# Attention row sums on VectorE and GpSimd, with P^T stored chunk-innermost, in place of ones-matmuls on TensorE

## The chip, the cores and the metric

The kernel runs on one core of one Trainium2 chip. The metric is the device time of one execution in microseconds (us), as the median of several executions. The profile's span is a little shorter than that time (366.2 us against 368.0 us for the profiled execution of the kernel before), because it runs from the first to the last instruction.

## The reference, cut to what matters

Two independent problems A and B, each a grouped-query attention block with a cache:

```python
# B=16, Sq=32, D=1024, Hq=32, Hkv=4, Sk=512, Dh=128, all bf16
q = (x @ wq)                                  # 32 query heads of 128
scores = einsum("bhqd,bhkd->bhqk", q, k) * Dh ** -0.5   # 8 query heads share one k head
p = softmax(scores, axis=-1)
o = einsum("bhqk,bhkd->bhqd", p, v)
out = o.reshape(B, Sq, Hq * Dh) @ wo          # both problems concatenated on the last axis
```

## The kernel before

The kernel works in 128 slots, one for each (batch, key head) of both problems. A slot holds the scores transposed: the 512 keys lie on the 128 partitions in KC = 4 chunks, and the QW = 256 columns are 8 heads x 32 queries. So a softmax row sum is a sum over 4 chunks and over 128 partitions. P^T below is the tile `p_sb`, the exponentials in this transposed form. In `nc.tensor.matmul` the `lhsT` argument is called the stationary operand and `rhs` the moving operand; SBUF and PSUM are the names of the two memories in which the kernel places its tiles. Around the attention work of a slot, TensorE is fed with seven "units", single 512-column matmuls of the projections (Q first, then the output projection).

```python
def scores(i):
    ...
    s_ps = psum.tile([P, KC, QW], FP32, name="s_ps", tag="s")
    for c in range(KC):
        nc.tensor.matmul(s_ps[:, c, :], lhsT=kT[:, i % GRP, c, :], rhs=<q of the 8 heads>, ...)
    p_sb = work.tile([P, KC, QW], BF16, name="p_sb", bufs=3)         # chunk-outermost
    nc.scalar.activation(out=p_sb[:], in_=s_ps[:], func=ACTF.Exp, bias=shift[:], scale=SCALE)

def partial_sums(i):                       # VectorE: sum of the 4 chunks
    nc.vector.tensor_tensor(out=t1[:], in0=p_sb[:, 0:2, :], in1=p_sb[:, 2:4, :], op=ALU.add)
    nc.vector.tensor_tensor(out=t[:], in0=t1[:, 0, :], in1=t1[:, 1, :], op=ALU.add)

def values(i):
    ob = psum.tile([P, 2 * QW], FP32, name="ob", tag="ob")
    for c in range(KC):
        nc.tensor.matmul(ob[:, 0:QW], lhsT=v_sb[:, i % GRP, c, :], rhs=d["p"][:, c, :], ...)
    nc.tensor.matmul(ob[:, QW:2 * QW], lhsT=ones[:], rhs=d["t"][:], start=True, stop=True)  # sum over partitions
    nc.scalar.activation(out=lg[:, q, :], in_=ob[:, QW:2 * QW], func=ACTF.Ln)
    nc.scalar.activation(out=r[:], in_=lg[:, q, :], func=ACTF.Exp, scale=-1.0)              # 1 / sum
    ...

for i in range(2 * NG):                    # 128 slots
    do_loads(i); scores(i); run(units, 4)
    if i > 0: values(i - 1)
    partial_sums(i); run(units, 3)
    if i > 0: normalize(i - 1)             # VectorE: ob * r -> oT
```

At the end a check value is read and a branch skips a slow general path, which these inputs never take.

Of the kernel before, what the change touches and what calls it, by code (L numbers as in the profile page):

```python
# [24 lines left out]
SHIFT = 44.0  # L25
ONES = 2.0 ** -75
LIMIT = 20.0
# [145 lines left out]
def kernel(  # L173
# [26 lines left out]
    BPT = P // SQ  # L200
    QW = REP * SQ

    out_flat = out.flatten_outer_dims()
# [5 lines left out]
    def fast_path(ok_i):  # L209
        with ExitStack() as fctx:  # L210
            enter = fctx.enter_context
            const = enter(tc.tile_pool(name="const", bufs=1))
            blk = enter(tc.tile_pool(name="blk", bufs=20))
            kv = enter(tc.tile_pool(name="kv", bufs=2))
# [3 lines left out]
            enter(tc.manual_schedule())  # L218

            nc.scalar.preload_act_table_set("natural_log_exp_and_others")  # L220

# [3 lines left out]
            ident = const.tile([P, P], BF16, name="ident")  # L225
            make_identity(nc, ident[:])
            ones_f = const.tile([P, P], FP32, name="ones_f")
            nc.vector.memset(ones_f[:], ONES)
            ones = const.tile([P, P], FP32R, name="ones")
            nc.vector.tensor_copy(out=ones[:], in_=ones_f[:])  # L230
            one_col = const.tile([P, 1], FP32, name="one_col")
# [4 lines left out]
            nc.vector.memset(cnt[:], 0.0)  # L236
            NLR = 2 * NG // GRP
            lall = const.tile([NLR, GRP * QW], FP32, name="lall")

# [25 lines left out]
            def load_kv(j):  # L265
                pr, jj = divmod(j, NG // GRP)
                k, v = problems[pr][1], problems[pr][2]
                kT = kv.tile([P, GRP, SK], BF16, name="kT")
                v_sb = kv.tile([P, GRP, KC, DH], BF16, name="v_sb")
                if pr == 0:  # L270
                    g, b0 = divmod(jj * GRP, B)
                    ks, vs = k[b0:b0 + GRP, g], v[b0:b0 + GRP, g]
                    for q in range(GRP):
                        nc.sync.dma_start_transpose(out=kT[:, q, :], in_=ks[q])
                else:
                    ks, vs = k[jj], v[jj]
                    nc.sync.dma_start_transpose(
                        out=kT[:], in_=ks.rearrange("g k d -> (g k) d")
                    )
                nc.sync.dma_start(  # L280
                    out=v_sb[:], in_=vs.rearrange("q (p c) d -> p q c d", c=KC)
                )
                kv_tiles[j] = (kT, v_sb)
# [26 lines left out]

            def f_units(pr, tt, nh, last=False):
                ps = psum.tile([P, NW], FP32, name="f_ps", tag="proj")
                for h in range(HQ):
                    nc.tensor.matmul(  # L314
                        ps[:],
                        lhsT=oT[pr, tt][:, h, :],
                        rhs=wo_tiles[pr, nh, h // REP][:, h % REP, :],
                        start=(h == 0),
                        stop=(h == HQ - 1),
                    )  # L320
                    if h == HQ - 1:
                        o_sb = outp.tile([P, NW], BF16, name="o_sb")
                        nc.vector.tensor_copy(out=o_sb[:], in_=ps[:])  # L323
                        c0 = problems[pr][5] + nh * NW
                        (nc.sync if last else nc.gpsimd).dma_start(  # L325
                            out=out_flat[tt * P:(tt + 1) * P, c0:c0 + NW], in_=o_sb[:]
                        )
                    yield
# [16 lines left out]
            def scores(i):  # L345
# [3 lines left out]
                for c in range(KC):  # L349
# [6 lines left out]
                    )  # L356
                p_sb = work.tile([P, KC, QW], BF16, name="p_sb", bufs=3)
                nc.scalar.activation(  # L358
                    out=p_sb[:], in_=s_ps[:], func=ACTF.Exp, bias=shift[:], scale=SCALE
                )  # L360
                st[i] = {"p": p_sb}

            def partial_sums(i):
                p_sb = st[i]["p"]
                t1 = work.tile([P, 2, QW], FP32, name="t1")
                nc.vector.tensor_tensor(
                    out=t1[:], in0=p_sb[:, 0:2, :], in1=p_sb[:, 2:4, :], op=ALU.add
                )
                t = work.tile([P, QW], FP32R, name="t")
                nc.vector.tensor_tensor(  # L370
                    out=t[:], in0=t1[:, 0, :], in1=t1[:, 1, :], op=ALU.add
                )
                st[i]["t"] = t

            ltile = {}

            def values(i):
                d = st[i]
                v_sb = kv_tiles[i // GRP][1]
                ob = psum.tile([P, 2 * QW], FP32, name="ob", tag="ob")  # L380
                for c in range(KC):
                    nc.tensor.matmul(  # L382
                        ob[:, 0:QW],
                        lhsT=v_sb[:, i % GRP, c, :],
                        rhs=d["p"][:, c, :],
                        start=(c == 0),
                        stop=(c == KC - 1),
                    )
                nc.tensor.matmul(  # L389
                    ob[:, QW:2 * QW], lhsT=ones[:], rhs=d["t"][:], start=True, stop=True  # L390
                )
                d["ob"] = ob
                j, q = divmod(i, GRP)
                if q == 0:
                    ltile[j] = work.tile([P, GRP, QW], FP32, name="lg")
                lg = ltile[j]
                nc.scalar.activation(  # L397
                    out=lg[:, q, :], in_=ob[:, QW:2 * QW], func=ACTF.Ln
                )
                r = work.tile([P, QW], FP32, name="r")  # L400
                nc.scalar.activation(out=r[:], in_=lg[:, q, :], func=ACTF.Exp, scale=-1.0)  # L401
                d["r"] = r
                if q == GRP - 1:
                    nc.gpsimd.dma_start(  # L404
                        out=lall[j:j + 1, :],
                        in_=lg[0:1, :, :].rearrange("p q n -> p (q n)"),
                    )

            def normalize(i):
                pr, b, g = where(i)  # L410
                d = st.pop(i)
                tt, bl = divmod(b, BPT)
                if (pr, tt) not in oT:
                    oT[pr, tt] = blk_tile([P, HQ, P], "oT")
                nc.vector.scalar_tensor_tensor(  # L415
                    out=oT[pr, tt][:, g * REP:(g + 1) * REP, bl * SQ:(bl + 1) * SQ],
                    in0=d["r"][:].rearrange("p (h s) -> p h s", s=SQ),
                    scalar=ONES,
                    in1=d["ob"][:, 0:QW].rearrange("p (h s) -> p h s", s=SQ),
                    op0=ALU.mult,  # L420
                    op1=ALU.mult,
                )
# [70 lines left out]
            def stream():  # L493
# [4 lines left out]
                for nh in range(NH):  # L498
                    for tt in range(TT):
                        yield from f_units(0, tt, nh)  # L500
                for tts in ((0, 1), (2,)):
                    for nh in range(NH):
                        for tt in tts:
                            yield from f_units(1, tt, nh)
                for nh in range(NH):
                    yield from f_units(1, TT - 1, nh, last=(nh == NH - 1))

# [9 lines left out]
            for j in range(2, 2 * NG // GRP):  # L517
                at(GRP * (j - 1) + 1, load_kv, j)
            for c4 in range(3, 16):
# [7 lines left out]
            at(12, load_xT_b)  # L527
            for nh in range(NH):
                for hg in range(HKV):
                    at(NG - 12 + nh * 8 + hg * 2, load_wo, 0, nh, hg)  # L530
                    at(NG + 20 + nh * 18 + hg, load_wo, 1, nh, hg)

# [4 lines left out]

            for i in range(2 * NG):
                do_loads(i)
                scores(i)  # L540
                run(units, 4)
                if i > 0:
                    values(i - 1)
                partial_sums(i)
                run(units, 3)
                if i > 0:
                    normalize(i - 1)
            run(units, 4)
            values(2 * NG - 1)
            run(units, 4)  # L550
            normalize(2 * NG - 1)


            run(units, 8)
            sq = blk_tile([NLR, GRP * QW], "sq", FP32)
            nc.vector.tensor_tensor(out=sq[:], in0=lall[:], in1=lall[:], op=ALU.mult)
# [15 lines left out]
                        skip_runtime_bounds_check_because="only compared")  # L572
    with tc.If(ok < total, preferred_fallthrough_block=False):
        general_path(tc, problems, out_flat)
# [30 lines left out]
```

## Time and profile before

| what | before |
|---|---|
| time, median | 368.9 us (at the prediction: 368.77 us) |
| PE busy | 97% of the span |
| VectorE, ScalarE busy | 67%, 68% |
| slot period (timeline) | 2.52 us |

The page of the kernel before: its first part (busy us, share, instructions), its part 4 (the chain that ended last, by engine), and rows of its part 5 (line, engine, operation, out<-in, count, busy us, mean ns of one).

```profile
PE 356.6 (97%) x2236; PEld 225.0 (61%) x2236; DVE 244.2 (67%) x478; ACT 249.2 (68%) x389; POOL 25.1 (7%) x53
...
PE 97%; DVE 0%; ACT 0%; issue 0%
...
L358 ACT ACTIVATE p_sb<-s_ps,shift 128x1024 bf16<-128x1024 f32 x128 | 142.7, 1115 | 47.5 <-PE s_ps L350 47.5
...
L382 PE MATMUL ob<-p_sb,v_sb 128*128 128x256 bf16 x512 | 76.8, 273 | 0.0
L350 PE MATMUL s_ps<-qT,kT 128*128 128x256 bf16 x512 | 76.8, 273 | 0.0
...
L389 PE MATMUL ob<-t,ones 128*128 128x256 f32 x128 | 46.5, 363 | 0.0
```

The timeline of PE in the kernel before (start us, duration us of the merged run, engine, line, operation, count).

```profile
200.36 0.60 PE L350 MATMUL s_ps<-qT,kT 128*128 128x256 bf16 x4
200.80 1.03 PE L314 MATMUL f_ps<-wo_sb,oT 128*128 128x512 bf16 x4
201.66 0.60 PE L382 MATMUL ob<-p_sb,v_sb 128*128 128x256 bf16 x4
202.02 0.36 PE L389 MATMUL ob<-t,ones 128*128 128x256 f32 x1
202.22 0.82 PE L314 MATMUL f_ps<-wo_sb,oT 128*128 128x512 bf16 x3
202.88 0.60 PE L350 MATMUL s_ps<-qT,kT 128*128 128x256 bf16 x4
```

How to read this: a matmul's mean of 273 ns is how long one takes, but they are pipelined, and what counts is the distance between starts. Four score matmuls occupy the array from 200.36 to 200.80, 0.44 us, 0.11 us each; four value matmuls and the ones-matmul together occupy 201.66 to 202.22, 0.56 us. One slot lasts from 200.36 to 202.88, 2.52 us. PE never waits in the loop (its only wait is 1.2 us, at the start), so TensorE is the bound. Busy time is a poor measure of what matmuls cost here: the ones-matmuls' 46.5 us of busy time are 4.2% of the chain, 15.4 us.

VectorE had one reducing instruction of the size that the change needs, 1024 elements, at the end of the kernel before (timeline of DVE):

```profile
349.40 1.21 DVE L557 TENSOR_SCALAR_CACHE_REDUCE sq<-sq 32x1024 f32<-32x1024 f32 x1
```

### The profile page before, as it was taken

The page shows a single profiled execution, that of the slowest core. Times are in us where ns is not written, and L with a number is a line of the kernel's source. Part 1 is how long each engine was busy: PE and PEld are TensorE (multiplying, and loading weights), DVE is VectorE, ACT ScalarE, POOL GpSimd, SP SyncE. Part 2 cuts the span into 40 slices and gives each one's busy share as a digit, 9 for nine tenths or more (in the row PEclk, how much of TensorE's full clock was granted, in tenths as well). Part 3 has the DMA queues.
Part 4 walks back from the last instruction along what each step waited for, and adds up shares of the span by engine and source line. Part 5 has one row for each costly group of instructions (what it writes and reads, how often), then busy time and mean ns, then how long its engine had stood idle before and what let it go on. Part 6 is the DMA issues. An engine that isn't in the chain of part 4 may idle for free.

```text
span 366.2 us, 6094 instructions
## 1 busy us (share of the span) xinstructions
PE 356.6 (97%) x2236; PEld 225.0 (61%) x2236; DVE 244.2 (67%) x478; ACT 249.2 (68%) x389; POOL 25.1 (7%) x53
## 2 busy tenths in 40 slices
PE   8999999999999999999999999999999999999990
PEld 5556666666666666666666666666666666666540
DVE  2458788887878787888856666666666676666530
ACT  3037777777777777777777777777777777777500
POOL 0000000000000000000001110110001111011100
PEclk9999999999999999999999999999999999999998
DMA  8998796977777784999995555799548974440000
GB/s 274 301 280 242 225 264 147 243 225 219 184 194 183 220 201 115 314 304 310 314 305 138 130 131 142 207 352 198 139 113 287 315 194 117 131 129 17 15 16 21
DMA packets 125974, 71.91 MB, mean 196 GB/s; under 512 B 74641, under 2 KB 124945, under 8 KB 125937
## 3 DMA queue, kind: packets, MB, share of 16 engines
q1 hardware_dynamic: 122848, 68.30, 67.5%
q0 software_dynamic: 1744, 2.10, 2.4%
q10 hardware_dynamic: 1344, 1.05, 0.9%
q8 instruction: 19, 0.31, 0.4%
q14 instruction: 19, 0.15, 0.1%
HBM read 51.38 MB, written 2.10 MB: 146 GB/s over the span
## 4 chain that ended last, share of the span: by engine, by line
PE 97%; DVE 0%; ACT 0%; issue 0%
PE f_ps L314 31%; PE q_ps L297 30%; PE s_ps L350 15%; PE ob L382 15%; PE ob L389 4%; PE warm_ps L446 1%; PE q_ps L469 1%; PE xT_ps L455 0%; ACT xT L460 0%; DVE o_sb L323 0%; DVE xT L459 0%; DVE warm L224 0%; PE ok_ps L563 0%
## 5 line engine op out<-in xcount | busy, mean ns | idle before, releaser
L358 ACT ACTIVATE p_sb<-s_ps,shift 128x1024 bf16<-128x1024 f32 x128 | 142.7, 1115 | 47.5 <-PE s_ps L350 47.5
L314 PE MATMUL f_ps<-wo_sb,oT 128*128 128x512 bf16 x512 | 132.8, 380 | 0.0
L297 PE MATMUL q_ps<-xT,wq_sb 128*128 128x512 bf16 x496 | 128.4, 380 | 0.0
L382 PE MATMUL ob<-p_sb,v_sb 128*128 128x256 bf16 x512 | 76.8, 273 | 0.0
L350 PE MATMUL s_ps<-qT,kT 128*128 128x256 bf16 x512 | 76.8, 273 | 0.0
L397 ACT ACTIVATE lg<-ob 128x256 f32<-128x256 f32 x128 | 49.5, 387 | 39.8 <-PE ob L389 39.8
L350 PEld LDWEIGHTS <-kT 128*128 128x128 bf16 x512 | 57.0, 113 | 28.3 <-issue 0.2
L382 PEld LDWEIGHTS <-v_sb 128*128 128x128 bf16 x512 | 50.1, 98 | 33.1
L314 PEld LDWEIGHTS <-oT 128*128 128x128 bf16 x512 | 44.6, 98 | 32.9
L297 PEld LDWEIGHTS <-wq_sb 128*128 128x128 bf16 x496 | 43.4, 97 | 31.9
L401 ACT ACTIVATE r<-lg 128x256 f32<-128x256 f32 x128 | 53.6, 418 | 4.0
L305 DVE CAST qT<-q_ps 128x512 bf16<-128x512 f32 x62 | 42.7, 689 | 18.2 <-PE q_ps L297 18.0
L415 DVE SCALAR_TENSOR_TENSOR oT<-r,ob 128x256 bf16<-128x256 f32 x128 | 53.5, 418 | 1.6 <-ACT r L401 1.6
L389 PE MATMUL ob<-t,ones 128*128 128x256 f32 x128 | 46.5, 363 | 0.0
L404 POOL DMA_DIRECT2D lall<-lg x32 | 15.9, 496 | 245.4 <-ACT lg L397 245.4
L389 PEld LDWEIGHTS ob<-t,ones 128*128 128x128 f32 x128 | 24.3, 190 | 1.4
L323 DVE CAST o_sb<-f_ps 128x512 bf16<-128x512 f32 x16 | 11.0, 689 | 9.0 <-PE f_ps L314 9.0
L325 POOL DMA_DIRECT2D out_dram<-o_sb x15 | 8.6, 571 | 81.3 <-DVE o_sb L323 81.3
L460 ACT COPY xT<-xT_ps 128x512 bf16<-128x512 bf16 x4 | 2.1, 590 | 5.1 <-DVE xT L459 5.1
L459 DVE COPY xT<-xT_ps 128x512 bf16<-128x512 bf16 x4 | 1.7, 426 | 5.3 <-PE xT_ps L455 5.3
L446 PE MATMUL warm_ps<-warm 128*128 128x512 bf16 x10 | 4.0, 560 | 1.2 <-DVE warm L224 1.2
L469 PE MATMUL q_ps<-xT,wq_sb 128*128 128x256 bf16 x32 | 4.0, 272 | 0.1
(280 smaller groups left out, 158.5 us busy)
## 6 DMA issues: line engine op xcount, KB each, us to landing
v_sb<-in_A_v_cache_dram SPq DMA_DIRECT2D x16, 512.0 KB, 4.2
wq_sb<-in_B_wq_dram SPq DMA_DIRECT2D x8, 1024.0 KB, 6.3
wo_sb<-in_A_wo_dram SPq DMA_DIRECT2D x8, 1024.0 KB, 7.5
v_sb<-in_B_v_cache_dram SPq DMA_DIRECT2D x16, 512.0 KB, 4.2
wo_sb<-in_B_wo_dram SPq DMA_DIRECT2D x8, 1024.0 KB, 8.9
wq_sb<-in_A_wq_dram SPq DMA_DIRECT2D x7, 1024.0 KB, 7.1
out_dram<-o_sb POOLq DMA_DIRECT2D x15, 128.0 KB, 2.4
kT<-in_A_k_cache_dram SPq DMA_TRANSPOSE x64, 3.1
```

The costliest lines, as they stand in the source:

```text
L297: nc.tensor.matmul(ps[:], lhsT=w[:, dc, (h % 4) * DH:(h % 4 + 1) * DH], rhs=xT[pr][:, dc, :], start=(dc == 0), stop=(dc == DC - 1),)
L305: nc.vector.tensor_copy(out=qT[pr, g][:, :, hl, :], in_=ps[:].rearrange("p (b s) -> p b s", s=SQ),)
L314: nc.tensor.matmul(ps[:], lhsT=oT[pr, tt][:, h, :], rhs=wo_tiles[pr, nh, h // REP][:, h % REP, :], start=(h == 0), stop=(h == HQ - 1),)
L323: nc.vector.tensor_copy(out=o_sb[:], in_=ps[:])
L350: nc.tensor.matmul(s_ps[:, c, :], lhsT=kT[:, i % GRP, c, :], rhs=qT[pr, g][:, b, :, :].rearrange("p h s -> p (h s)"), start=True, stop=True,)
L358: nc.scalar.activation(out=p_sb[:], in_=s_ps[:], func=ACTF.Exp, bias=shift[:], scale=SCALE)
L382: nc.tensor.matmul(ob[:, 0:QW], lhsT=v_sb[:, i % GRP, c, :], rhs=d["p"][:, c, :], start=(c == 0), stop=(c == KC - 1),)
L389: nc.tensor.matmul(ob[:, QW:2 * QW], lhsT=ones[:], rhs=d["t"][:], start=True, stop=True)
L397: nc.scalar.activation(out=lg[:, q, :], in_=ob[:, QW:2 * QW], func=ACTF.Ln)
L401: nc.scalar.activation(out=r[:], in_=lg[:, q, :], func=ACTF.Exp, scale=-1.0)
L404: nc.gpsimd.dma_start(out=lall[j:j + 1, :], in_=lg[0:1, :, :].rearrange("p q n -> p (q n)"),)
L415: nc.vector.scalar_tensor_tensor(out=oT[pr, tt][:, g * REP:(g + 1) * REP, bl * SQ:(bl + 1) * SQ], in0=d["r"][:].rearrange("p (h s) -> p h ...
```

## The change

The intent is to take the ones-matmul off the bound engine. P^T is stored with the four chunks innermost, `[P, QW, KC]`, so that VectorE sums the chunks in one reduce over contiguous elements; GpSimd, almost idle before, sums over the partitions for two slots at a time; Ln and the reciprocal run once for two slots; the value matmuls and everything that waits for the sums run four slots behind (LAG = 4). The value matmuls must then read every fourth bf16 element of P^T, a step of 8 bytes. Besides, the last output is written in two halves, the branch at the end gets a hint, the identity matrix is built on VectorE instead of GpSimd, the logarithms kept for the check are stored from ScalarE's queue, and loads are scheduled a little differently.

```diff
-                p_sb = work.tile([P, KC, QW], BF16, name="p_sb", bufs=3)
+                p_sb = work.tile([P, QW, KC], BF16, name="p_sb", bufs=LAG + 2)
                 nc.scalar.activation(
-                    out=p_sb[:], in_=s_ps[:], func=ACTF.Exp, bias=shift[:], scale=SCALE
+                    out=p_sb[:], in_=s_ps[:].rearrange("p c n -> p n c"), func=ACTF.Exp, bias=shift[:], scale=SCALE
                 )
 ...
-                nc.vector.tensor_tensor(
-                    out=t1[:], in0=p_sb[:, 0:2, :], in1=p_sb[:, 2:4, :], op=ALU.add
-                )
 ...
-                nc.vector.tensor_tensor(
-                    out=t[:], in0=t1[:, 0, :], in1=t1[:, 1, :], op=ALU.add
-                )
 ...
+                nc.vector.tensor_reduce(
+                    out=tsum[j][:, q, :],
+                    in_=p_sb[:],
+                    axis=AX.X,
+                    op=ALU.add,
+                )
+                if q == 1:
+                    sums[j] = work.tile([P, 2, QW], FP32, name="sums", bufs=3)
+                    nc.gpsimd.partition_all_reduce(
+                        sums[j][:].rearrange("p q n -> p (q n)"),
+                        tsum.pop(j)[:].rearrange("p q n -> p (q n)"),
+                        channels=P,
+                        reduce_op=bass_isa.ReduceOp.add,
+                    )
 ...
+            def reciprocals(j):
+                lg = sums.pop(j)
+                nc.scalar.activation(out=lg[:], in_=lg[:], func=ACTF.Ln, scale=DOWN)
+                rcp[j] = work.tile([P, 2, QW], FP32, name="r")
+                nc.scalar.activation(out=rcp[j][:], in_=lg[:], func=ACTF.Exp, scale=-1.0)
 ...
                     nc.tensor.matmul(
-                        ob[:, 0:QW],
+                        ob[:],
                         lhsT=v_sb[:, i % GRP, c, :],
-                        rhs=d["p"][:, c, :],
+                        rhs=st[i]["p"][:, :, c],
 ...
-                nc.tensor.matmul(
-                    ob[:, QW:2 * QW], lhsT=ones[:], rhs=d["t"][:], start=True, stop=True
-                )
 ...
-                for nh in range(NH):
-                    yield from f_units(1, TT - 1, nh, last=(nh == NH - 1))
+                yield from f_units(1, TT - 1, 0, NW, nc.gpsimd)
+                yield from f_units(1, TT - 1, NW, QW, nc.sync)
+                yield from f_units(1, TT - 1, NW + QW, QW, nc.scalar)
 ...
-    with tc.If(ok < total, preferred_fallthrough_block=False):
+    with tc.If(ok < total, preferred_fallthrough_block=True, label="general"):
```

More of the change, by code (lines that the diff above doesn't have):

```diff
@@ L4 @@
 import concourse.tile as tile
-from concourse import bass_utils, mybir
+from concourse import bass_isa, bass_utils, mybir
 from concourse._compat import with_exitstack
@@ L25 @@
 SHIFT = 44.0
-ONES = 2.0 ** -75
+DOWN = 2.0 ** -75
 LIMIT = 20.0
@@ L201 @@
     QW = REP * SQ
+    LAG = 4
     out_flat = out.flatten_outer_dims()
@@ L212, in fast_path @@
             const = enter(tc.tile_pool(name="const", bufs=1))
-            blk = enter(tc.tile_pool(name="blk", bufs=20))
+            blk = enter(tc.tile_pool(name="blk", bufs=19))
             kv = enter(tc.tile_pool(name="kv", bufs=2))
@@ L218, in fast_path @@
             enter(tc.manual_schedule())
+            tc.mark_branch_hint_location(
+                "general",
+                "LikelyTaken",
+                [nc.sync.engine, nc.scalar.engine, nc.vector.engine, nc.tensor.engine, nc.gpsimd.engine],
+            )
             nc.scalar.preload_act_table_set("natural_log_exp_and_others")
@@ L225, in fast_path @@
             ident = const.tile([P, P], BF16, name="ident")
-            make_identity(nc, ident[:])
-            ones_f = const.tile([P, P], FP32, name="ones_f")
-            nc.vector.memset(ones_f[:], ONES)
-            ones = const.tile([P, P], FP32R, name="ones")
-            nc.vector.tensor_copy(out=ones[:], in_=ones_f[:])
+            col = const.tile([P, P], BF16, name="col")
+            row = const.tile([P, P], BF16, name="row")
+            nc.vector.memset(row[:], 1.0)
+            nc.vector.tensor_tensor_scan(
+                out=col[:], data0=row[:], data1=row[:], initial=0.0, op0=ALU.mult, op1=ALU.add
+            )
+            nc.vector.transpose(out=row[:], in_=col[:])
+            nc.vector.memset(ident[:], 0.0)
+            for k in range(0, P, 32):
+                d = slice(k, k + 32)
+                nc.vector.tensor_tensor(
+                    out=ident[d, d], in0=row[d, d], in1=col[d, d], op=ALU.is_equal
+                )
             one_col = const.tile([P, 1], FP32, name="one_col")
@@ L236, in fast_path @@
             nc.vector.memset(cnt[:], 0.0)
-            NLR = 2 * NG // GRP
-            lall = const.tile([NLR, GRP * QW], FP32, name="lall")
+            NLR = NG
+            lall = const.tile([NLR, 2 * QW], FP32, name="lall")
             def blk_tile(shape, name, dtype=BF16):
@@ L268, in load_kv @@
                 kT = kv.tile([P, GRP, SK], BF16, name="kT")
-                v_sb = kv.tile([P, GRP, KC, DH], BF16, name="v_sb")
+                v_sb = kv.tile([P, GRP, KC, DH], BF16, name="v_sb", bufs=3)
                 if pr == 0:
@@ L309, in q_units, with f_units @@
                     yield
-            def f_units(pr, tt, nh, last=False):
+            def f_units(pr, tt, n0, width, eng):
                 ps = psum.tile([P, NW], FP32, name="f_ps", tag="proj")
+                nh, off = divmod(n0, NW)
                 for h in range(HQ):
                     nc.tensor.matmul(
-                        ps[:],
+                        ps[:, 0:width],
                         lhsT=oT[pr, tt][:, h, :],
-                        rhs=wo_tiles[pr, nh, h // REP][:, h % REP, :],
+                        rhs=wo_tiles[pr, nh, h // REP][:, h % REP, off:off + width],
                         start=(h == 0),
@@ L322, in f_units @@
                         o_sb = outp.tile([P, NW], BF16, name="o_sb")
-                        nc.vector.tensor_copy(out=o_sb[:], in_=ps[:])
-                        c0 = problems[pr][5] + nh * NW
-                        (nc.sync if last else nc.gpsimd).dma_start(
-                            out=out_flat[tt * P:(tt + 1) * P, c0:c0 + NW], in_=o_sb[:]
+                        if eng is nc.scalar:
+                            nc.scalar.copy(out=o_sb[:, 0:width], in_=ps[:, 0:width])
+                        else:
+                            nc.vector.tensor_copy(out=o_sb[:, 0:width], in_=ps[:, 0:width])
+                        c0 = problems[pr][5] + n0
+                        eng.dma_start(
+                            out=out_flat[tt * P:(tt + 1) * P, c0:c0 + width],
+                            in_=o_sb[:, 0:width],
                         )
@@ L356, in scores @@
                     )
-                p_sb = work.tile([P, KC, QW], BF16, name="p_sb", bufs=3)
+                p_sb = work.tile([P, QW, KC], BF16, name="p_sb", bufs=LAG + 2)
                 nc.scalar.activation(
-                    out=p_sb[:], in_=s_ps[:], func=ACTF.Exp, bias=shift[:], scale=SCALE
+                    out=p_sb[:], in_=s_ps[:].rearrange("p c n -> p n c"), func=ACTF.Exp, bias=shift[:], scale=SCALE
                 )
                 st[i] = {"p": p_sb}
+            tsum, sums, logs, rcp = {}, {}, {}, {}
@@ L363, in partial_sums @@
             def partial_sums(i):
                 p_sb = st[i]["p"]
-                t1 = work.tile([P, 2, QW], FP32, name="t1")
-                nc.vector.tensor_tensor(
-                    out=t1[:], in0=p_sb[:, 0:2, :], in1=p_sb[:, 2:4, :], op=ALU.add
-                )
-                t = work.tile([P, QW], FP32R, name="t")
-                nc.vector.tensor_tensor(
-                    out=t[:], in0=t1[:, 0, :], in1=t1[:, 1, :], op=ALU.add
-                )
-                st[i]["t"] = t
@@ L375, in fast_path @@
-            ltile = {}
+                j, q = divmod(i, 2)
+                if q == 0:
+                    tsum[j] = work.tile([P, 2, QW], FP32, name="t")
+                nc.vector.tensor_reduce(
[3 more added lines that the diff above has]
+                    op=ALU.add,
+                )
+                if q == 1:
[5 more added lines that the diff above has]
+                        reduce_op=bass_isa.ReduceOp.add,
+                    )
@@ new lines, in reciprocals, with keep_logs @@
+            def reciprocals(j):
[3 more added lines that the diff above has]
+                nc.scalar.activation(out=rcp[j][:], in_=lg[:], func=ACTF.Exp, scale=-1.0)
+                logs[j] = lg
+            def keep_logs(j):
+                nc.scalar.dma_start(
+                    out=lall[j:j + 1, :],
+                    in_=logs.pop(j)[0:1, :, :].rearrange("p q n -> p (q n)"),
+                )
@@ L377, in values @@
             def values(i):
-                d = st[i]
                 v_sb = kv_tiles[i // GRP][1]
-                ob = psum.tile([P, 2 * QW], FP32, name="ob", tag="ob")
+                ob = psum.tile([P, QW], FP32, name="ob", tag="ob")
                 for c in range(KC):
                     nc.tensor.matmul(
-                        ob[:, 0:QW],
+                        ob[:],
                         lhsT=v_sb[:, i % GRP, c, :],
-                        rhs=d["p"][:, c, :],
+                        rhs=st[i]["p"][:, :, c],
@@ L388, in values @@
                     )
-                nc.tensor.matmul(
-                    ob[:, QW:2 * QW], lhsT=ones[:], rhs=d["t"][:], start=True, stop=True
-                )
-                d["ob"] = ob
-                j, q = divmod(i, GRP)
-                if q == 0:
-                    ltile[j] = work.tile([P, GRP, QW], FP32, name="lg")
-                lg = ltile[j]
-                nc.scalar.activation(
-                    out=lg[:, q, :], in_=ob[:, QW:2 * QW], func=ACTF.Ln
-                )
-                r = work.tile([P, QW], FP32, name="r")
-                nc.scalar.activation(out=r[:], in_=lg[:, q, :], func=ACTF.Exp, scale=-1.0)
-                d["r"] = r
-                if q == GRP - 1:
-                    nc.gpsimd.dma_start(
-                        out=lall[j:j + 1, :],
-                        in_=lg[0:1, :, :].rearrange("p q n -> p (q n)"),
-                    )
+                st[i]["ob"] = ob
             def normalize(i):
@@ L416, in normalize @@
                     out=oT[pr, tt][:, g * REP:(g + 1) * REP, bl * SQ:(bl + 1) * SQ],
-                    in0=d["r"][:].rearrange("p (h s) -> p h s", s=SQ),
-                    scalar=ONES,
-                    in1=d["ob"][:, 0:QW].rearrange("p (h s) -> p h s", s=SQ),
+                    in0=rcp[i // 2][:, i % 2, :].rearrange("p (h s) -> p h s", s=SQ),
+                    scalar=DOWN,
+                    in1=d["ob"][:].rearrange("p (h s) -> p h s", s=SQ),
                     op0=ALU.mult,
@@ L499, in stream @@
                     for tt in range(TT):
-                        yield from f_units(0, tt, nh)
+                        yield from f_units(0, tt, nh * NW, NW, nc.gpsimd)
                 for tts in ((0, 1), (2,)):
@@ L503, in stream @@
                         for tt in tts:
-                            yield from f_units(1, tt, nh)
-                for nh in range(NH):
-                    yield from f_units(1, TT - 1, nh, last=(nh == NH - 1))
+                            yield from f_units(1, tt, nh * NW, NW, nc.gpsimd)
+                yield from f_units(1, TT - 1, 0, NW, nc.gpsimd)
+                yield from f_units(1, TT - 1, NW, QW, nc.sync)
+                yield from f_units(1, TT - 1, NW + QW, QW, nc.scalar)
             units = stream()
@@ L517, in fast_path @@
             for j in range(2, 2 * NG // GRP):
-                at(GRP * (j - 1) + 1, load_kv, j)
+                at(GRP * (j - 1), load_kv, j)
             for c4 in range(3, 16):
@@ L527, in fast_path @@
             at(12, load_xT_b)
-            for nh in range(NH):
-                for hg in range(HKV):
-                    at(NG - 12 + nh * 8 + hg * 2, load_wo, 0, nh, hg)
-                    at(NG + 20 + nh * 18 + hg, load_wo, 1, nh, hg)
+            for hg in range(HKV):
+                at(52 + 2 * hg, load_wo, 0, 0, hg)
+                at(68 + 4 * hg, load_wo, 0, 1, hg)
+                at(85 + 4 * hg, load_wo, 1, 0, hg)
+                at(104 + 2 * hg, load_wo, 1, 1, hg)
             def do_loads(i):
@@ L535, in do_loads @@
                     fn(*args)
-            for i in range(2 * NG):
-                do_loads(i)
-                scores(i)
-                run(units, 4)
-                if i > 0:
-                    values(i - 1)
-                partial_sums(i)
-                run(units, 3)
-                if i > 0:
-                    normalize(i - 1)
-            run(units, 4)
-            values(2 * NG - 1)
-            run(units, 4)
-            normalize(2 * NG - 1)
+            total_slots = 2 * NG
+            for i in range(total_slots + LAG):
+                live = i < total_slots
+                if live:
+                    do_loads(i)
+                    scores(i)
+                if i % 2 == 1 and i >= 3:
+                    if i >= 5:
+                        keep_logs(i // 2 - 2)
+                    if i // 2 - 1 < NG:
+                        reciprocals(i // 2 - 1)
+                run(units, 4 if live else 5)
+                if i >= LAG:
+                    values(i - LAG)
+                if live:
+                    partial_sums(i)
+                run(units, 3 - (i % 4 == 3) if live else 3)
+                if i >= LAG:
+                    normalize(i - LAG)
             run(units, 8)
-            sq = blk_tile([NLR, GRP * QW], "sq", FP32)
+            sq = blk_tile([NLR, 2 * QW], "sq", FP32)
             nc.vector.tensor_tensor(out=sq[:], in0=lall[:], in1=lall[:], op=ALU.mult)
```

## The prediction

> **What bounds the kernel now.** TensorE. The page has PE busy 356.6 us of 366.2 (97%); the chain of waits is PE for 97%; the wait view shows PE waiting once, 1.2 us at the start; the granted clock is 1.00. The timeline repeats every 2.52 us per (batch, head-group) slot: seven projection matmuls of 512 columns (1.51 us), four score matmuls (0.44), then four value matmuls and the ones-matmul, together 0.56. VectorE is busy 32.1 of 40 us in the Q-projection stage and about 25.4 in the output stage; ScalarE 30.5; GpSimd almost idle.
>
> **What the change removes.** 128 ones-matmuls. Their busy time (46.5 us, 363 ns each) is latency, not rate. If four value matmuls take 0.44 us like four score matmuls, a ones-matmul costs 0.12 us of PE time; the chain agrees: 4.2% of the span, 15.4 us, all on the critical path. Two VectorE adds per slot (0.69 + 0.43 us) go too.
>
> **What it adds or moves (estimates from the trace).**
> - VectorE: one reduce of 1024 elements per slot. The existing 1024-element reducing instruction takes 1.21 us; so 1.21 against 1.12. VectorE needs about 2.1 us of a 2.40 us slot in the Q stage (~89%): no bound, little slack.
> - ScalarE: Ln and Exp on 512 columns every second slot (about 0.63 us each): slightly less work. The big Exp (1.12 us) now reads PSUM strided; I assume the same duration.
> - GpSimd: 64 all-sums of 128x512. No trace has their duration. Budget: 4.8 us (two slots) for throughput; about 3.5 us before Ln waits; the lag of 4 slots absorbs about 1 us more. I expect 2.5-4 us, hidden. [...]
> - PE: value matmuls read P^T with an 8-byte step. [...] The trace shows only a stationary operand with that step (weight loads 113 ns against 98). I expect 273 ns to stay.
> - Tail: the last output is split in halves and the branch hinted: last cast 0.69 -> ~0.4 us, smaller last store, perhaps 1 us of branch: 1-2 us together. The identity moves from GpSimd to VectorE, under the warm-up: no change.
> - DMA: 0.95 busy at 140-180 us; a faster loop asks 5% more there; earlier K/V issue and spread weight loads should cover it. Allowance for new small waits: about 0.5 us.
>
> **Sum.** 368.8 - 15.4 - 1.5 + ~0.5 = about 352.0 us. Range 348.5 to 362. Faster by over 2%: 0.81; within 2%: 0.11; slower: 0.08.
>
> **What would show it.** Slot period 2.40 us; PE still ~97% busy, the chain still PE; no ones row; value matmuls at 273 ns; the reduce at 1.2 us; the big Exp at 1.1; all-sums below 4 us with Ln scarcely waiting for GpSimd; a shorter end after the last matmul.
>
> **What would make it wrong.** Value matmuls slowed by the step (each +25% is 14 us); the strided Exp near 2 us, making ScalarE the bound; an all-sum over 4.8 us (each 0.1 us above costs 6 us); VectorE stretched by GpSimd traffic past its 0.3 us slack, so that PSUM frees late; DMA starving K/V around slots 52-60.

The 2.5 to 4 us of an all-sum and the 1 us of the branch were estimates.

## The result and the profile after

The changed kernel takes 407.36 us (median of 4), against 368.89 us before: it is slower. The ratio is 1.1045, with a 95% interval of 1.1026 to 1.1064. Here and below a ratio is the mean time of one kernel's fast runs over that of the other's fast runs of the same rounds, so it is not quite the ratio of the medians quoted.

The page of the changed kernel, the same parts as of before.

```profile
PE 400.5 (99%) x2140; PEld 223.6 (55%) x2140; DVE 254.5 (63%) x356; ACT 220.5 (54%) x262; POOL 214.7 (53%) x83
...
PE 99%; ACT 0%; DVE 0%; issue 0%; DVEq 0%
...
L397 POOL PARTITION_ALL_REDUCE sums<-t x64 | 206.8, 3230 | 160.5 <-DVE t L389 119.8
L377 ACT ACTIVATE p_sb<-s_ps,shift 128x1024 bf16<-128x1024 f32 x128 | 142.6, 1114 | 149.4 <-PE s_ps L369 149.4
L389 DVE TENSOR_REDUCE t<-p_sb 128x256 f32<-128x1024 bf16 x128 | 155.9, 1218 | 90.4 <-ACT p_sb L377 89.3
L421 PE MATMUL ob<-p_sb,v_sb 128*128 128x256 bf16 x512 | 136.6, 401 | 0.0
```

The timeline of PE in the changed kernel, then all that PE waited for in it (us in total, times, longest us).

```profile
121.54 1.07 PE L421 MATMUL ob<-p_sb,v_sb 128*128 128x256 bf16 x4
122.43 0.83 PE L311 MATMUL q_ps<-xT,wq_sb 128*128 128x512 bf16 x3
123.09 0.60 PE L369 MATMUL s_ps<-qT,kT 128*128 128x256 bf16 x4
123.53 1.03 PE L311 MATMUL q_ps<-xT,wq_sb 128*128 128x512 bf16 x4
124.39 1.07 PE L421 MATMUL ob<-p_sb,v_sb 128*128 128x256 bf16 x4
```

```profile
PE warm_ps L467 <- DVE warm L230: 1.3, 1, 1.3
```

TensorE is still the bound: PE is 99% busy, and the chain is PE. PE's only wait is 1.3 us at the start; in the loop it waits for none of the other engines. But four value matmuls now hold the array from 121.54 to 122.43, 0.89 us instead of about 0.44, and the slot takes 2.85 us (121.54 to 124.39) instead of 2.52. The score matmuls, of the same shape but with a contiguous moving operand, still take 0.44 us (123.09 to 123.53). "PE busy" cannot show this: a matmul that reads slowly is as busy as one that reads fast (PE 99% here, 97% before). The share of the weight loads does: PEld is 61% before, 55% here, and 61% again with the pair layout below (e3); but waiting lowers it too (56% in e1 below).

The end became shorter. The last output is issued at the times below; the span ends at 366.2 us before and at 406.0 us after, so 7.5 us and 3.8 us after the issue began. These are the timeline of SP in the kernel before, then that of ACT in the changed kernel.

```profile
358.67 0.36 SPq L325 DMA_DIRECT2D out_dram<-o_sb  x1
```

```profile
402.23 0.37 ACTq L343 DMA_DIRECT2D out_dram<-o_sb  x1
```

### The profile page after: what moved, and what is told of

It is laid out like the page before. It is cut to its first block, busy times and chain, and to the rows that moved or that the text cites. A ratio compares the mean times of both kernels' runs of the same rounds, so it can differ in the third digit from the quotient of the medians.

```text
span 406.0 us, 5615 instructions
## 1 busy us (share of the span) xinstructions
PE 400.5 (99%) x2140; PEld 223.6 (55%) x2140; DVE 254.5 (63%) x356; ACT 220.5 (54%) x262; POOL 214.7 (53%) x83
## 4 chain that ended last, share of the span: by engine, by line
PE 99%; ACT 0%; DVE 0%; issue 0%; DVEq 0%
PE ob L421 29%; PE f_ps L329 27%; PE q_ps L311 26%; PE s_ps L369 14%; PE warm_ps L467 1%; PE q_ps L490 1%; PE xT_ps L476 1%; ACT o_sb L339 0%; DVE warm L230 0%; PE ok_ps L591 0%; DVEq L628 0%
## 5 line engine op out<-in xcount | busy, mean ns | idle before, releaser
L397 POOL PARTITION_ALL_REDUCE sums<-t x64 | 206.8, 3230 | 160.5 <-DVE t L389 119.8
L377 ACT ACTIVATE p_sb<-s_ps,shift 128x1024 bf16<-128x1024 f32 x128 | 142.6, 1114 | 149.4 <-PE s_ps L369 149.4
L389 DVE TENSOR_REDUCE t<-p_sb 128x256 f32<-128x1024 bf16 x128 | 155.9, 1218 | 90.4 <-ACT p_sb L377 89.3
L421 PE MATMUL ob<-p_sb,v_sb 128*128 128x256 bf16 x512 | 136.6, 401 | 0.0
L329 PE MATMUL f_ps<-wo_sb,oT 128*128 128x512 bf16 (+1 forms) x544 | 133.0, 368 | 0.0
L421 PEld LDWEIGHTS <-v_sb 128*128 128x128 bf16 x512 | 54.5, 107 | 58.7
L329 PEld LDWEIGHTS <-oT 128*128 128x128 bf16 x544 | 55.3, 102 | 42.8
L311 PEld LDWEIGHTS <-wq_sb 128*128 128x128 bf16 x496 | 50.5, 102 | 42.9
L406 ACT ACTIVATE sums<-sums 128x512 f32<-128x512 f32 x64 | 39.8, 621 | 4.5 <-POOL sums L397 4.2
L408 ACT ACTIVATE r<-sums 128x512 f32<-128x512 f32 x64 | 40.5, 632 | 2.0
L341 DVE CAST o_sb<-f_ps 128x512 bf16<-128x512 f32 (+1 forms) x16 | 10.8, 672 | 10.3 <-PE f_ps L329 10.3
```

What stands on the lines that cost most here:

```text
L311: nc.tensor.matmul(ps[:], lhsT=w[:, dc, (h % 4) * DH:(h % 4 + 1) * DH], rhs=xT[pr][:, dc, :], start=(dc == 0), stop=(dc == DC - 1),)
L329: nc.tensor.matmul(ps[:, 0:width], lhsT=oT[pr, tt][:, h, :], rhs=wo_tiles[pr, nh, h // REP][:, h % REP, off:off + width], start=(h == 0), ...
L341: nc.vector.tensor_copy(out=o_sb[:, 0:width], in_=ps[:, 0:width])
L377: nc.scalar.activation(out=p_sb[:], in_=s_ps[:].rearrange("p c n -> p n c"), func=ACTF.Exp, bias=shift[:], scale=SCALE)
L389: nc.vector.tensor_reduce(out=tsum[j][:, q, :], in_=p_sb[:], axis=AX.X, op=ALU.add,)
L397: nc.gpsimd.partition_all_reduce(sums[j][:].rearrange("p q n -> p (q n)"), tsum.pop(j)[:].rearrange("p q n -> p (q n)"), channels=P, reduc ...
```

## The experiments

The theory: the 8-byte step of the moving operand alone halves the rate at which TensorE reads P^T, and everything else in the change hides as it was meant to. The first rival: the reads are slow because something else is in the way of SBUF, namely the new GpSimd all-sums or the VectorE reduce. The second rival, from the prediction itself: something besides the value matmuls has a cost (GpSimd and VectorE holding each other up, late sums, DMA), and the loss would be there without the step as well.

### e2_step_only: the step alone, in the kernel before

```diff
-                p_sb = work.tile([P, KC, QW], BF16, name="p_sb", bufs=3)
+                p_sb = work.tile([P, QW, KC], BF16, name="p_sb", bufs=3)
-                    out=p_sb[:], in_=s_ps[:], func=ACTF.Exp, bias=shift[:], scale=SCALE
+                    out=p_sb[:], in_=s_ps[:].rearrange("p c n -> p n c"), func=ACTF.Exp, bias=shift[:], scale=SCALE
-                    out=t1[:], in0=p_sb[:, 0:2, :], in1=p_sb[:, 2:4, :], op=ALU.add
+                    out=t1[:].rearrange("p c n -> p n c"), in0=p_sb[:, :, 0:2], in1=p_sb[:, :, 2:4], op=ALU.add
-                        rhs=d["p"][:, c, :],
+                        rhs=d["p"][:, :, c],
```

> The kernel before with one thing of the change alone: P^T chunk-innermost, so that the value matmuls read with an 8-byte step; the ones-matmuls, the two adds and ScalarE's small steps stay, and GpSimd does no all-sum. Theory (the step alone): four value matmuls take 0.89 us instead of 0.44, 0.45 us x 128 = 57 us more, about 426 us. Rival (GpSimd or the reduce disturbs TensorE): about 369 us. The strided Exp should stay near 1.11 us either way.

Measured: 428.47 us against 368.50 us, ratio 1.163 (1.1611 to 1.1649); the result is correct. A row of the page and the timeline of PE:

```profile
L382 PE MATMUL ob<-p_sb,v_sb 128*128 128x256 bf16 x512 | 137.1, 402 | 0.0
```

```profile
252.53 1.07 PE L382 MATMUL ob<-p_sb,v_sb 128*128 128x256 bf16 x4
253.24 0.48 PE L389 MATMUL ob<-t,ones 128*128 128x256 f32 x1
253.56 0.82 PE L314 MATMUL f_ps<-wo_sb,oT 128*128 128x512 bf16 x3
```

The value matmuls take 402 ns here too, though GpSimd makes no all-sum and VectorE no reduce. The value and ones-matmuls together last 1.03 us (252.53 to 253.56) instead of 0.56. The step alone costs 428.5 - 368.5 = 60.0 us, close to the 57 us expected (1.03 - 0.56 = 0.47 us a slot, 128 times, is 60). The strided Exp takes 1113 ns, as before. The first VectorE add, which here reads pairs that stand 8 bytes apart and writes its two halves 1 KiB apart, slowed from 0.69 to 1.08 us, which is hidden, because PE still does not wait for VectorE in the loop (its only wait is 1.2 us, at the start).

### e5_step_sweep and e9_sweep_warm: the cost of a step, measured by itself

In both, extra matmuls of 256 columns stand after the first two heads of the kernel before, when GpSimd has nothing to do and VectorE only two casts, during the first group. They read the transposed x of problem A as one long row; their result is never used.

```diff
             first_heads(1, 1)
+            xflat = xT[0][:].rearrange("p c n -> p (c n)")
+            for _ in range(24):        # the same again for steps 2, 3, 4, 5, 6, 8 and 16, each on its own line
+                nc.tensor.matmul(warm_ps[:, 0:256], lhsT=warm[:, 0:P], rhs=xflat[:, 0:256:1], start=True, stop=True)
```

> The kernel before with 8 stretches of 24 extra matmuls of 256 columns after the first two heads, reading the transposed x with steps of 1, 2, 3, 4, 5, 6, 8 and 16 elements while VectorE and GpSimd do nothing. Theory (the step alone): step 1 starts every 0.107-0.11 us, step 4 every 0.22 us. [...] Rival (disturbance by other engines): all steps alike. The whole run is longer by the sum of the stretches, 20 us if all are at full rate and some 40 us if most are at half.

Measured (a single execution of 421.46 us): the timeline of PE, steps 1, 2, 3 and 4, and the first line of step 5.

```profile
10.97 2.79 PE L495 MATMUL warm_ps<-xT,warm 128*128 128x256 bf16 x24
13.59 2.88 PE L497 MATMUL warm_ps<-xT,warm 128*128 128x256 bf16 x24
16.32 4.29 PE L499 MATMUL warm_ps<-xT,warm 128*128 128x256 bf16 x24
20.44 5.61 PE L501 MATMUL warm_ps<-xT,warm 128*128 128x256 bf16 x24
25.87 6.98 PE L503 MATMUL warm_ps<-xT,warm 128*128 128x256 bf16 x24
```

The distance between two group starts, divided by 24, is the time of one matmul: 0.109 us at step 1 (2.62 / 24), 0.114 at step 2, 0.172 at step 3, 0.226 at step 4. The granted clock was 1.00 up to step 5, but 0.64 during step 6 and 0.50 during steps 8 and 16. (The 0.64 is a mean: finer windows show 1.00 until 35 us and 0.50 from there. PE is 100% busy throughout; why the clock fell is not shown.) So a second sweep put 32 matmuls of step 1 after each group of 8; there the clock was 1.00 in six of eight windows of about 10 us, and 0.86 and 0.97 in the other two.

> The step sweep again, because in the first one the granted clock had fallen to 0.64 at step 6 and 0.50 at steps 8 and 16: steps 4, 5, 6, 8, 12 and 16, in groups of 8 matmuls, each group followed by 32 matmuls with step 1 that keep the array busy. If the first sweep's times came from the reading of SBUF: 0.226, 0.283, 0.340 and 0.453 us at steps 4, 5, 6, 8, and no more than about 0.46 at 12 and 16, at a granted clock near 1. If the clock made the large steps slow: 8, 12 and 16 come out faster than 0.45.

Measured (a single execution of 447.79 us): the timeline of PE, one group of step 8 and one of step 16, each with the line that follows it.

```profile
46.03 3.78 PE L520 MATMUL warm_ps<-xT,warm 128*128 128x256 bf16 x8
49.63 3.68 PE L522 MATMUL warm_ps<-xT,warm 128*128 128x256 bf16 x32
...
76.09 3.84 PE L536 MATMUL warm_ps<-xT,warm 128*128 128x256 bf16 x8
79.75 3.67 PE L538 MATMUL warm_ps<-xT,warm 128*128 128x256 bf16 x32
```

| step, bf16 elements | bytes | us per 256-column matmul | against step 1 |
|---|---|---|---|
| 1 | 2 | 0.109 | 1.0 |
| 2 | 4 | 0.114 | 1.04 |
| 3 | 6 | 0.172 | 1.6 |
| 4 | 8 | 0.226 (second sweep 0.224) | 2.1 |
| 5, 6 | 10, 12 | 0.283, 0.340 (second sweep 0.282, 0.338) | 2.6, 3.1 |
| 8 | 16 | 0.450 (second sweep) | 4.1 |
| 12, 16 | 24, 32 | 0.446, 0.458 (second sweep) | 4.1, 4.2 |

Up to 4 bytes a step is nearly free (0.114 us against 0.109). From there the time grows with the bytes covered (0.172 us at 6 bytes, 0.450 at 16), and above 16 bytes it grows no more (0.446 us at 24, 0.458 at 32). The clock is not the cause: at a granted clock of 0.50 steps 8 and 16 took 0.453 and 0.460 us in the first sweep ((51.70 - 40.83) / 24 and (62.74 - 51.70) / 24), against 0.450 and 0.458 at 1.00 in the second. Matmuls of step 1 were slower at a lower clock: the one group of 32 in which it fell, to a mean of 0.67, took 0.162 us each instead of 0.110.

From 4 to 16 bytes, 0.028 us for each byte of the step fits the times to within 0.004 us (0.028 x 6 = 0.168 at step 3, 0.028 x 16 = 0.448 at step 8); this is an estimate fitted to the table, and what in the reading causes it is not shown. At a step of 8 bytes the moving operand of a bf16 matmul is read at half rate (0.226 us), at 4 bytes within 5% of the full one (0.114 us). VectorE, ScalarE and GpSimd are busy 0.00 us from 14 to 62 us of the first sweep, so the first rival falls here as well. DMA was moving data during steps 1 to 5, but none during steps 8 and 16.

### e1_contiguous_p: the changed kernel without the step

```diff
-                p_sb = work.tile([P, QW, KC], BF16, name="p_sb", bufs=LAG + 2)
+                p_sb = work.tile([P, KC, QW], BF16, name="p_sb", bufs=LAG + 2)
-                    out=p_sb[:], in_=s_ps[:].rearrange("p c n -> p n c"), func=ACTF.Exp, bias=shift[:], scale=SCALE
+                    out=p_sb[:], in_=s_ps[:], func=ACTF.Exp, bias=shift[:], scale=SCALE
-                    in_=p_sb[:],
+                    in_=p_sb[:].rearrange("p c n -> p n c"),
-                        rhs=st[i]["p"][:, :, c],
+                        rhs=st[i]["p"][:, c, :],
```

> The changed kernel with P^T chunk-outermost again: value matmuls read contiguous columns, the Exp is contiguous, and the VectorE reduce reads the four chunks through a view with a step of 512 bytes. Theory (the 8-byte step of the moving operand halves the rate of the value matmuls, everything else hides): value matmuls back to about 273 ns and 0.44 us per four, slot about 2.40 us, about 350 us in all if the reduce keeps near 1.2 us; if the stepped reduce takes over 1.5 us, VectorE becomes the bound, and the time is above that. Rival (the GpSimd all-sums or the VectorE reduce slow TensorE's reads of SBUF): value matmuls stay near 400 ns and the time near 407 us.

Measured: 383.71 us against 368.50 us, ratio 1.0414 (1.0397 to 1.0432); correct. From its page (busy, chain, groups), then the timeline of DVE.

```profile
PE 350.4 (92%) x2140; PEld 213.4 (56%) x2140; DVE 335.1 (88%) x356; ACT 215.1 (56%) x262; POOL 214.8 (56%) x83
...
DVE 56%; PE 13%; ACT 11%; issue 11%; POOL 6%; SPq 1%; DMA 1%; ACTq 0%; DVEq 0%; POOLq 0%
...
L389 DVE TENSOR_REDUCE t<-p_sb 128x256 f32<-128x1024 bf16 x128 | 247.3, 1933 | 13.2 <-ACT p_sb L377 13.2
...
L421 PE MATMUL ob<-p_sb,v_sb 128*128 128x256 bf16 x512 | 76.7, 272 | 10.7 <-DVE oT L436 9.4
```

```profile
120.05 1.91 DVE L389 TENSOR_REDUCE t<-p_sb 128x256 f32<-128x1024 bf16 x1
121.89 0.40 DVE L436 SCALAR_TENSOR_TENSOR oT<-r,ob 128x256 bf16<-128x256 f32 x1
122.22 0.67 DVE L319 CAST qT<-q_ps 128x512 bf16<-128x512 f32 x1
122.82 1.93 DVE L389 TENSOR_REDUCE t<-p_sb 128x256 f32<-128x1024 bf16 x1
```

The value matmuls are back at 272 ns, with the all-sums and a reduce still running beside them, so neither of these disturbs TensorE. But the same reduce now takes 1.93 us instead of 1.22, since the four inputs of each sum lie 512 bytes apart. VectorE has no gap left (2.77 us from reduce to reduce, 120.05 to 122.82), becomes the bound, and PE begins to wait for it. So the layout of P^T sets the speed of two readers that want opposite things: TensorE wants columns close together (272 ns a matmul at a step of 2 bytes, 401 at 8), the reduce wants chunks close together (1.22 us adjacent, 1.93 us 512 bytes apart).

### e3_pairs: a layout that serves both readers

Two chunks lie innermost and two outermost. TensorE then reads with a step of 4 bytes, and the reduce runs over pairs.

```diff
-                p_sb = work.tile([P, QW, KC], BF16, name="p_sb", bufs=LAG + 2)
+                p_sb = work.tile([P, 2, QW, 2], BF16, name="p_sb", bufs=LAG + 2)
-                    out=p_sb[:], in_=s_ps[:].rearrange("p c n -> p n c"), func=ACTF.Exp, bias=shift[:], scale=SCALE
+                    out=p_sb[:], in_=s_ps[:].rearrange("p (a b) n -> p a n b", b=2), func=ACTF.Exp, bias=shift[:], scale=SCALE
-                    in_=p_sb[:],
-                    axis=AX.X,
+                    in_=p_sb[:].rearrange("p a n b -> p n a b"),
+                    axis=AX.XY,
-                        rhs=st[i]["p"][:, :, c],
+                        rhs=st[i]["p"][:, c // 2, :, c % 2],
```

> The changed kernel with two chunks innermost and two outermost: the value matmuls read with a 4-byte step, the reduce runs over two inner axes. If any step above one element halves the rate: near 407 us. If the cost begins only above 4 bytes: value matmuls at 273 ns, slot about 2.40 us, about 350 us. If the cost grows with the bytes covered: in between.

Measured: 350.54 us against 368.50 us, ratio 0.9516 (0.9500 to 0.9533); correct. It beats both kernels. From its page, then the timeline of PE.

```profile
PE 341.9 (98%) x2140; PEld 213.1 (61%) x2140; DVE 251.2 (72%) x356; ACT 217.7 (63%) x262; POOL 214.5 (62%) x83
...
L389 DVE TENSOR_REDUCE t<-p_sb 128x256 f32<-128x1024 bf16 x128 | 155.8, 1217 | 56.9 <-ACT p_sb L377 55.7
...
L421 PE MATMUL ob<-p_sb,v_sb 128*128 128x256 bf16 x512 | 78.9, 275 | 0.2 <-DVE oT L436 0.2
```

```profile
121.58 0.62 PE L421 MATMUL ob<-p_sb,v_sb 128*128 128x256 bf16 x4
122.03 0.81 PE L311 MATMUL q_ps<-xT,wq_sb 128*128 128x512 bf16 x3
...
123.98 0.62 PE L421 MATMUL ob<-p_sb,v_sb 128*128 128x256 bf16 x4
```

The value matmuls take 0.45 us per four, the reduce keeps its 1.217 us, and the slot is 2.40 us (121.58 to 123.98), as the prediction had it for the changed kernel. Pairs are enough for VectorE too: runs of two bf16 elements, 4 bytes, were as fast as four adjacent ones (1217 ns against 1218). PE's waits in the loop sum to 0.6 us. Four small edits are the whole difference between 407.4 and 350.5 us.

### e8_no_allsum: does GpSimd cost anything?

The pair layout without the all-sum: each partition's own sum goes on to Ln. The result is wrong. (The edit against the changed kernel has the four lines of e3 too, and gives the tile `t` four buffers instead of two.)

```diff
-                    sums[j] = work.tile([P, 2, QW], FP32, name="sums", bufs=3)
-                    nc.gpsimd.partition_all_reduce(...)
+                    sums[j] = tsum.pop(j)
```

> The pair layout without the all-sum: ScalarE takes each partition's own sum (a wrong result, on purpose), so GpSimd does only its stores and nothing waits for it. If the all-sums are hidden and disturb nobody, the time stays at 350.5 us within 0.5%. If they cost by contention or by late Ln, it falls by the cost.

Measured: 350.27 us, against 350.54 us with the all-sums (kernel before 368.63 and 368.50 us). The ratios to the kernel before, 0.9504 (0.9488 to 0.9520) and 0.9516 (0.9500 to 0.9533), overlap, so the 64 all-sums of 3.23 us each are hidden to within a few tenths of a per cent in the pair layout. The second rival falls for GpSimd. For the changed kernel itself the wait view above says the same: PE waits for nothing in its loop.

### e4_two_adds: does it matter how VectorE sums?

This was tried as a better version: contiguous P^T for TensorE, and the two adds of the kernel before instead of the reduce.

```diff
 (the contiguous layout of e1, and)
-                nc.vector.tensor_reduce(out=tsum[j][:, q, :], in_=p_sb[:], axis=AX.X, op=ALU.add)
+                t1 = work.tile([P, 2, QW], FP32, name="t1", bufs=1)
+                nc.vector.tensor_tensor(out=t1[:], in0=p_sb[:, 0:2, :], in1=p_sb[:, 2:4, :], op=ALU.add)
+                nc.vector.tensor_tensor(out=tsum[j][:, q, :], in0=t1[:, 0, :], in1=t1[:, 1, :], op=ALU.add)
```

> The changed kernel with P^T chunk-outermost (value matmuls contiguous) and VectorE's sum made by the two adds of the kernel before instead of the reduce; GpSimd's all-sum stays. If the adds keep their 0.69 and 0.43 us beside a busy GpSimd: slot 2.39 us, value matmuls 0.44 us per four instead of 0.455 in the pair layout, so about 348.5 us, some 2 us below the pair layout's 350.5. If GpSimd and two-input adds hold each other up [...]: the adds take clearly longer than 0.69 and 0.43 us, or the all-sum clearly longer than 3.23, and where VectorE or GpSimd passes its slack the time is above 350.5.

Measured: 385.89 us against 368.63 us, ratio 1.0465 (1.0448 to 1.0483); correct. The timeline of DVE, then that of POOL.

```profile
121.02 2.19 DVE L390 TENSOR_TENSOR t<-p_sb 128x512 f32<-128x512 bf16 x1
123.32 0.43 DVE L393 TENSOR_TENSOR t<-t 128x256 f32<-128x256 f32 x1
...
124.59 0.68 DVE L390 TENSOR_TENSOR t<-p_sb 128x512 f32<-128x512 bf16 x1
```

```profile
120.42 3.23 POOL L398 PARTITION_ALL_REDUCE sums<-t  x1 [2.33 <-ACT p_sb L377]
125.99 3.23 POOL L398 PARTITION_ALL_REDUCE sums<-t  x1 [2.33 <-ACT p_sb L377]
```

The add at 121.02 starts while an all-sum runs and takes 2.19 us; the one at 124.59 stands between two all-sums and takes 0.68, as in the kernel before. The mean of all 128 is 1.47 us. VectorE is then 86% busy on average, and PE (92%) waits for it. The reduce, and the other VectorE instructions of the loop, read at most one tensor from SBUF and keep their times beside the all-sum: with it (e3) and without it (e8) the reduce takes 1217 and 1218 ns, the product into `oT` 410 and 411, the cast into `qT` 685 and 687. Not every two-input add is slowed: the second one, at 123.32, starts in the last 0.33 us of the all-sum and keeps its 0.43 us. The first add ends 2.79 us after the start of the all-sum, whether it begins 0.60 us into it, as here, or 0.03 us into it (at 131.58 beside the all-sum of 131.55, where it takes 2.76 us). That looks as if it were held until about 2.1 us into the all-sum and then ran its 0.68 us; this is inferred from the ends, not shown. What in the first add causes it, its two SBUF inputs or something else, was not tested by itself. So the reduce, which looks like an even trade for the two adds (1.22 against 1.12 us), is what lets the all-sum run beside VectorE at little cost (350.54 us with it, 350.27 without, e8): the same layout with the reduce (e1) has its own price, and of the layouts tried only that of e3 avoids both.

### e6_hint and e7_hint_halves: the end of the kernel

The first adds the hinted branch to the kernel before, the second also the last output in halves.

```diff
+            tc.mark_branch_hint_location("general", "LikelyTaken", [<all five engines>])
-    with tc.If(ok < total, preferred_fallthrough_block=False):
+    with tc.If(ok < total, preferred_fallthrough_block=True, label="general"):
```

> The kernel before with the branch hint and the turned branch alone. If the hint is what shortens the end after the last matmul from 8.2 us in the profile of before to 4.2 in that of the changed kernel, it saves 2.5 to 3.5 us: about 365.5 us. If it is nothing: 368.5.

> The kernel before with the branch hint and the last output in two halves of 256 columns, on the SyncE and the ScalarE queue: the whole tail part of the change, and nothing else. Expected some 4 us below before, about 364.5 us, of which 0.5 to 1 us come from the halves.

Measured: 365.45 us with the hint (ratio 0.9912, 0.9896 to 0.9929) and 364.87 us with hint and halves (0.9892, 0.9875 to 0.9909), against 368.63 us. The branch, hint and turned condition together, saves 3.2 us. The halves seem to save 0.6 us more, but the two intervals overlap, so that part is not settled.

## Why the prediction was wrong

- **The step that failed.** The prediction said of the value matmuls: "I expect 273 ns to stay." They take 401 ns, and 0.89 us per four instead of 0.44. That alone is worth 60.0 us (e2), and it turned an expected gain of 17 us into a loss of 38.5. The risk was named first among those that could make the prediction wrong, with the right size (14 us for each 25%), but at far too low a chance (0.08 for slower): that the step costs nothing was an assumption, and the trace of before held no moving operand with a step to show it. The one hint that it did hold, stationary loads with the same step at 113 ns against 98, was read as harmless.
- **What the change removes was right.** The prediction had 15.4 us for the ones-matmuls. From e2 (step, with ones-matmuls) to the changed kernel (step, without) the time falls by 428.5 - 407.4 = 21.1 us; 3.8 of this is the end (e7), which leaves about 17 us, an estimate, since the two kernels differ in other small things too.
- **VectorE was right.** The reduce was put at 1.21 us and takes 1.218, and VectorE is no bound in the changed kernel (63% busy) nor with pairs (72%).
- **ScalarE was right.** The strided Exp takes 1114 ns against 1115; Ln and Exp on 512 columns take 0.62 and 0.63 us, as estimated (a line through 387 ns for Ln on 256 columns and 1115 ns for Exp on 1024, both in the kernel before, gives 0.63).
- **GpSimd was right.** The all-sum takes 3.23 us, inside the 2.5 to 4 us expected, and it is hidden (e8). That VectorE sums with the reduce and not with the two adds turned out to be essential: beside an all-sum the reduce kept its 1.22 us (e3), while the first add took 2.19 us instead of 0.68 (e4).
- **The end was mis-sized.** 1 to 2 us were expected; the hint and the halves save 3.8 us (e7), nearly all of it the branch.
- **DMA was right as far as it goes.** PE waits for no load in the loop of the changed kernel. In the faster kernel with pairs the PE waits sum to 0.6 us.
- **The sum.** Without the failed step the prediction would have held: the pair layout, which takes only that step away, runs in 350.5 us against 352.0 predicted. That it is so close is in part luck: the end gave 2.3 us more than the 1.5 us entered for it.
- **The signs named.** "PE still ~97% busy, the chain still PE" came true (99%) while the time went the wrong way, so it was no test. The signs that did tell were the slot period (2.85 us for 2.40) and the mean of the value matmuls (401 ns for 273).

## What to carry to other kernels

When a layout is changed to suit one reader, list every other reader of the tile and measure each at its new step; a few dozen extra matmuls in an idle stretch cost one run and give the whole curve. Here TensorE kept its rate up to a 4-byte step (0.114 us for 256 columns, against 0.109) and lost half of it at 8 bytes (0.226 us), while a VectorE reduce was content with pairs (1217 ns, against 1218), so the layout between the two extremes won. To see a slow operand in a trace, compare distances between starts of like-shaped matmuls, not PE's busy share (0.89 us against 0.44 per four here, at 99% and 97% busy).
